# Chunk-selected attention into a softplus MLP on one core: constant rows cleared on GpSimd and written in pieces, key copies moved to GpSimd

## The chip, the cores and the metric

The kernel runs on one core of a Trainium2 chip. The metric is device time in microseconds (us); the time given for a kernel is the median over several runs, and one more execution is taken with the hardware profiler.

The engines are named here as the profile names them: PE is TensorE (PEld its weight loads), DVE is VectorE, ACT is ScalarE, POOL is GpSimd, SP is SyncE, which here issues DMAs alone.

## The reference

Inputs are q, k and v of shape 4 x 8 x 768 x 64 (batch, heads, tokens, head size), `w_in` of 512 x 2048 and `w_out` of 2048 x 512, all float32.

```
k_min, k_max = min, max of k over chunks of 32 tokens           # 24 chunks
ub    = sum_d max(q * k_min, q * k_max)                         # a bound for each query and chunk
ub    = -1e9 where the chunk lies after the query's own chunk
sel   = the 6 chunks with the largest ub, for each query
s     = q k^T / 8, kept where the key's chunk is in sel and the key is not after the query
attn  = softmax(s) v                                            # 4 x 8 x 768 x 64
x     = attn, heads side by side                                # 3072 x 512
out   = softplus(x w_in) w_out                                  # 3072 x 512
```

## The kernel before

**Blocks.** Work is cut into 12 blocks of 256 queries, three for each of the four batches, numbered n = 0 to 11. A block is prepared (`prep`), attended in four pairs of heads p = 0 to 3 (`attend`), and goes through the MLP (`mlp_h`, `mlp_y`). Blocks 0, 1 and 2 (all of batch 0) are the ramp: nothing else is there yet to fill TensorE. From block 3 on, preparation and attention of block n + 3 are interleaved with the MLP of block n.

**Preparation.** In the ramp, TensorE transposes k (L537) and q (L605) into PSUM; VectorE takes minimum and maximum over the chunks (`kx`, L544), copies them into a block-diagonal tile `bd` (L588) and makes the positive and negative parts of q (`qp`, `qn`, L624). TensorE multiplies these into the bounds (L646, L647). VectorE adds the causal mask (L653), takes the largest eight (L662), compares with the sixth (L672) and writes a mask row (L675); TensorE transposes it (L691) and it is copied beside q (`ma`, L696).

**Selection inside the score matmul.** The mask is applied by the score matmul itself. The tiles `ka` and `kb` (one of each for even and odd batches, `i` = 0 and 1) hold the keys of the two heads of a pair on 64 partitions and, on 32 more, one-hot rows that tell each key's chunk. `ka` uses partitions 0 to 63 for the keys and 64 to 95 for the one-hot rows; `kb` has zeros on partitions 0 to 31, the one-hot rows on 32 to 63 and the keys on 64 to 127. One matmul over them gives score plus penalty (L775). These rows are constant: zeros (`kb0`, L371), one-hot rows from the tile `ohb` (L374 for batch 0, a DMA on GpSimd's queue, L377, for batch 1).

**Blocks 0 and 1 are special** (`NSPLIT` = 2). Their keys go whole into `ka` of batch 1, which is still free, and their scores are made by half-height matmuls, keys first (L749) and the one-hot part from `ohb` itself (L756). Block 2 needs the keys of blocks 0 and 1 in the proper tiles of batch 0, so eight copies of 64 x 512 bring them there (`kcp`, L556). Block 2 reads them, and the constant rows of batch 0, when its scores (L775) begin.

**Attention.** ScalarE takes exponentials of the scores (L785), GpSimd clears the causal triangle (L791), TensorE multiplies with V (L802), VectorE inverts the sums (L811) and scales (L823). In the ramp TensorE transposes the result (L831) and a copy puts it into `x` (L836). V is cast from float32 by GpSimd or, in the ramp, by GpSimd or ScalarE, whichever the planner finds free (L721).

**MLP.** TensorE makes x w_in (L859), ScalarE softplus as exponential (L865) and logarithm (L869), TensorE multiplies with w_out (L885), VectorE copies it out (L890).

**Order.** Every step is a task with an engine, an estimated duration, a priority and the keys that it reads and writes. A planner (`Graph.schedule`) plays these through and fixes the order of instructions on each engine when the kernel is built; on the chip each engine runs its list in order and waits on semaphores. Where the planner sees TensorE without work in its first 30 us it writes a dummy matmul into the list (L387, 128 x 256). `at=` keeps a task from starting before a planned time, `port=True` says that a VectorE task may not overlap a GpSimd one in the plan, `MOVES` takes named tasks out of the finished order and puts them behind others. `RLEAD`, `POST`, `SHIFT`, `PLEAD` and `MSTART` shift priorities.

**DMA queues.** SP loads q, k and v. GpSimd's queue loads `w_in` in two pieces (L466) and `w_out` in four (L469); each group stands behind a one-element copy (`holdp`, L478) that waits for earlier loads.

In the old order, VectorE runs L371, both L374 and the eight L556 in one row after block 1's mask copy, and L371 for batch 1 soon after.

Of the kernel before, what the change touches and what calls it, by code (L numbers as in the profile page):

```python
# [9 lines left out]
F32 = mybir.dt.float32  # L10
# [10 lines left out]
NP = H // 2  # L21
# [11 lines left out]
NRAMP = 3  # L33
NSPLIT = 2
SWITCH = 0.1
CPP = -12
LATE = 22
W2 = 18
WARM = 30.0
COLD = 4.2  # L40
TD = 1.9
TLAT = 1.4
RLEAD = (0, 1, -3)
POST = (2, 5, 3)
OPRIO = 25
LEAD = 14
BG = 40
DMA_START = 1.3
MSTART = 18
AOFF = 8  # L50
PADD = 0.0
PLEAD = 18
AEND = 20
ORDER = "k0 q0 k1 v0 q1 v1 i01 i23 k2 q2 v2 o0 o1 o2 o3".split()
HOLDS = [("q", 1, 1), ("q", 2, 1), ("q", 2, 1)]

READS = [("q", 1, 0), ("k", 2, 1)]
MOVES = [("holdp", 0, "vc0", 1), ("ldw_in", 0, "holdp", 0), ("ohka", 0, "vc2", 1), ("ohkb", 0, "ohka", 0)]
SHIFT = (0, 0, 8)


OWN = {"PE": 0.0, "ACT": 0.05, "DVE": 0.07, "POOL": 0.05, "SP": 0.0}
# [20 lines left out]
class Graph:  # L83
# [7 lines left out]
    def add(self, eng, dur, fn, prio, r=(), w=(), dma=None, lat=None, name="", after=(), pkt=18, port=None, alt=None, at=0.0):  # L91
        t = Task()
        t.n, t.eng, t.dur, t.fn, t.prio, t.dma, t.name = len(self.tasks), eng, dur, fn, prio, dma, name
        t.lat = LAT[eng] if lat is None else lat
        t.pkt = pkt
        t.half = False
        t.port = port if port is not None else eng == "POOL" and dma is None
        t.alts = {eng: (dur, fn, t.port)}
        if alt:
            t.alts[alt[0]] = (alt[1], alt[2], False)  # L100
        deps, bufs = set(after), []
        for key in list(r) + list(w):
            b = key[0] if isinstance(key, tuple) else key
            if isinstance(b, Buf) and b not in bufs:
                bufs.append(b)
        for key in r:
            if key in self.last:
                deps.add(self.last[key])
            self.readers.setdefault(key, []).append(t)
        for key in w:  # L110
            if key in self.last:
                deps.add(self.last[key])
            deps.update(x for x in self.readers.pop(key, ()) if x is not t)
            self.last[key] = t
        t.deps, t.users, t.bufs = deps, [], bufs
        for d in deps:
            d.users.append(t)
        for b in bufs:
            b.left += 1
        t.wait, t.ready, t.start, t.end, t.order = len(deps), at, None, None, None  # L120
        self.tasks.append(t)
        return t
# [167 lines left out]
def build(nc, tiles):  # L290
# [77 lines left out]
    def background(i, pr, after, blks):  # L368
        add("DVE", 0.2, lambda: DV.memset(T("bd", i), 0.0), pr, w=[("bd", i)], name="bd0", after=after)
        add("DVE", 0.1, lambda: DV.memset(T("v", i)[:, :, :, D:D + 1], 1.0), pr, w=[("v1", i)], name="v1", after=after)  # L370
        add("DVE", 1.35, lambda: DV.memset(T("kb", i)[0:32], 0.0), CPP2 if i == 0 else pr + 2, w=[("kb0", i)], name="kb0", after=after, at=LATE if i == 0 else 0.0)  # L371
        for which in ("ka", "kb"):
            if i == 0:
                add("DVE", 0.9, lambda which=which: DV.tensor_copy(*oh(which, i, blks)), CPP2, at=LATE, r=["ohb"], port=True,  # L374
                    w=[(which + "c", i, k_) for k_ in blks], name="oh" + which + "0", after=after)
                continue
            add("POOL", 0.6, lambda which=which: PO.dma_start(*oh(which, i, blks)), pr, r=["ohb"],  # L377
                w=[(which + "c", i, k_) for k_ in blks], name="oh" + which, after=after, dma=0.8, pkt=200, lat=0.7)

    for i in range(2):  # L380
        add("DVE", 0.5, lambda i=i: DV.memset(T("mr", i), 0.0), -8, w=[("mr0", i)], name="mr0")
    CPP2 = when_att[2, 0] + CPP
    background(0, -6, (), [0, 1, 2])


# [128 lines left out]
    def prep(n):  # L514
# [13 lines left out]
        if ramp:  # L528
            for hh in range(2):
                kT = ps("t")  # L530
                p2 = slice(hh * 2, hh * 2 + 2)

                def tr(hh=hh, kT=kT):
                    for p in range(2):
                        for t in range(NT):
                            c0 = (p * NT + t) * 128
                            PE.transpose(T(kT)[:, c0:c0 + 128], columns("k", n, hh, p, t), T("identf"))  # L537
                add("PE", 0.44, tr, pr + 0.01 * hh, r=landing("k", n, hh) + ["identf"], w=[kT], name=f"kT{n}")

                def kab(which, rs, kT=kT, p2=p2):  # L540
                    AC.copy(T(which, i)[rs, p2, ks_], T(kT)[rs].rearrange("d (p s) -> d p s", p=2))

                def red(m, kT=kT, p2=p2):
                    DV.tensor_reduce(T(kx)[:, m, p2],  # L544
                                     T(kT).rearrange("d (p c s) -> d p c s", p=2, s=CH), axis=AX.X,
                                     op=ALU.max if m == 0 else ALU.min, negate=m == 1)
                kr = add("DVE", 1.26, lambda red=red: (red(0), red(1)), pr + 0.1, r=[kT], w=[(kx, m, hh) for m in range(2)],
                    name=f"kx{n}")
                if split:

                    def kae(kT=kT, p2=p2):
                        AC.copy(T("ka", 1)[:, p2, ks_], T(kT).rearrange("d (p s) -> d p s", p=2))
                    add("ACT", 0.5, kae, pr + 0.2, r=[kT], w=[("ka", 1, j, hh) for j in js] + [("kac", 1, blk, hh)],
                        name=f"ka{n}", after=[kr] if n == 0 else ())
                    for which, rs in (("ka", slice(0, 64)), ("kb", slice(64, 128))):
                        add("DVE", 0.24, lambda which=which, rs=rs, p2=p2: DV.tensor_copy(  # L556
                            T(which, i)[rs, p2, ks_], T("ka", 1)[rs, p2, ks_]), when_att[2, 0] + CPP, at=LATE, port=True,
                            r=[("ka", 1, j, hh) for j in js] + [("kac", 1, blk)], w=[(which, i, j, hh) for j in js], name=f"kcp{n}")
                    continue
                add("ACT", 1.06, lambda kab=kab: (kab("ka", slice(0, 64)), kab("kb", slice(64, 128))), pr + 0.2, r=[kT],  # L560
                    w=[(w_, i, j, hh) for w_ in ("ka", "kb") for j in js], name=f"ka{n}")
        else:
            ks = KQ["k", n]
            kt = Buf("kt")

            def tr(ks=ks, kt=kt):
                SP.dma_start_transpose(T(kt), T(ks).rearrange("s p t c -> s (p t c)"))
            add("SP", TD, tr, pr, at=pr - 4, r=[(ks, 0), (ks, 1)], w=[kt], dma=1.25, lat=TLAT, name=f"kTd{n}")
            for m in range(2):
                def red(m=m, kt=kt):  # L570
                    DV.tensor_reduce(T(kx)[:, m].rearrange("d p (t c) -> d p t c", t=NT),  # L571
                                     T(kt).rearrange("d (p t) (c s) -> d p t c s", t=NT, s=CH),
                                     axis=AX.X, op=ALU.max if m == 0 else ALU.min, negate=m == 1)
                add("DVE", 1.13, red, pr + 1, r=[kt], w=[(kx, m, 0), (kx, m, 1)], name=f"kx{n}")

            def kab(which, rs, kt=kt):
                DV.tensor_copy(T(which, i)[rs, :, ks_].rearrange("d p (t s) -> d p t s", t=NT),
                               T(kt)[rs].rearrange("d (p t) s -> d p t s", t=NT))
            add("DVE", 0.36, port=True, fn=lambda: kab("ka", slice(0, 64)), prio=pr + 4, r=[kt],
                w=[("ka", i, j, hh) for j in js for hh in range(2)], name=f"ka{n}")  # L580
            add("DVE", 0.36, port=True, fn=lambda: kab("kb", slice(64, 128)), prio=pr + 4, r=[kt],
                w=[("kb", i, j, hh) for j in js for hh in range(2)], name=f"kb{n}")
# [134 lines left out]
        if ramp:  # L717
            for t in range(NT):
                xv = XF["v", n, t]
                def vc(eng, xv=xv, t=t):  # L720
                    return lambda: (PO.tensor_copy if eng else AC.copy)(  # L721
                        v_dst(n, t), T(xv).rearrange("s (h d) -> s h d", h=H))
                add("POOL", 0.6, vc(1), pr + 2, r=[(xv, 0), (xv, 1)], w=[("v", i, blk * NT + t)], name=f"vc{n}",
                    alt=("ACT", 0.52, vc(0)))


    OALL = {}
# [1 line left out]
    def attend(n, p):  # L729
# [32 lines left out]
        for h in range(2):  # L762
            pt = Buf("pt")
            pts.append(pt)
            for j in range(0, t0 + 2, 2):
# [10 lines left out]
                                  qq[r0:r1, p, q0:QB], start=True, stop=True)  # L776
                kn = "ka" if h == 0 else "kb"
                hh = p // 2
                r = [(kn, i, j, hh), (kn, i, j + 1, hh), (kn + "c", i, j // 2)] + ([("kb0", i)] if h else [])
                r += [(qb, hh, z) for z in range(3)] if h else [(qa, hh, z) for z in range(3)]  # L780
                if not halves:
                    add("PE", 0.166 if last else 0.22, sm, pr_s, r=r, w=[sp], name=f"s{n}")
# [239 lines left out]
```

## Time and profile before

| | us |
|---|---|
| median of 7 runs | 259.41 |
| lowest and highest | 258.95, 260.42 |
| the profiled execution, its own time | 259.29 |
| its span, first to last instruction | 257.6 |
| TensorE busy | 251.2 |
| ScalarE busy | 199.2 |
| VectorE busy | 151.7 |
| GpSimd busy | 83.5 |

All durations below come from the one profiled execution. A row of the order of time gives start, duration, engine, line, operation, output and input, and how many instructions are merged; what stands in brackets is how long the engine sat idle before it and who ended the wait. Starts count from the span's start.

### The profile page before, as it was taken

Reading aid. Unit: us, or ns where it says so; the run is one execution under the profiler, and the core shown is the slowest. Engines: PE = TensorE matmul, PEld = TensorE weight load, DVE = VectorE, ACT = ScalarE, POOL = GpSimd, SP = SyncE. Lnnn points to the kernel's source line nnn. Section 1 sums busy time; section 2 is a strip of 40 time slices with the busy share of each in tenths; the row PEclk is TensorE's granted clock in tenths of the full one; section 3 lists DMA queues with packets and bytes.
Section 4 is the critical chain, followed back from the end, with each engine's and each line's share of the span. In section 5 each row is a group of like instructions: output and inputs, shape, how many; then the busy total and the mean of one; then the engine's idle time right before and its main releaser. Section 6 shows DMA issues by size and latency. Waiting matters only on the chain.

```text
span 257.6 us, 6836 instructions
## 1 busy us (share of the span) xinstructions
PE 251.2 (98%) x2620; PEld 189.1 (73%) x2620; DVE 151.7 (59%) x555; ACT 199.2 (77%) x359; POOL 83.5 (32%) x176
## 2 busy tenths in 40 slices
PE   8999899999999999999999999999999999999994
PEld 6887696687685786877687778677677687685763
DVE  5897958458876993949896229486487310221101
ACT  2677989988494999899389879769689679796570
POOL 3352460256063470458223244323523001010000
PEclk9999999999999999999999999999999999999999
DMA  8999899999986969999963599744992310111202
GB/s 181 272 194 216 185 160 186 253 190 276 154 216 148 225 166 187 226 174 242 195 163 84 131 220 246 165 120 102 227 189 33 92 43 1 43 41 41 84 0 83
DMA packets 119897, 39.64 MB, mean 154 GB/s; under 512 B 113496, under 2 KB 115800, under 8 KB 119864
## 3 DMA queue, kind: packets, MB, share of 16 engines
q1 hardware_dynamic: 114456, 34.09, 61.3%
q0 software_dynamic: 3296, 4.59, 10.2%
q10 hardware_dynamic: 2112, 0.52, 0.9%
q8 instruction: 20, 0.33, 0.6%
q14 instruction: 13, 0.11, 0.1%
HBM read 27.26 MB, written 6.29 MB: 130 GB/s over the span
## 4 chain that ended last, share of the span: by engine, by line
PE 92%; DVE 6%; issue 1%; ACT 0%; DVEq 0%
PE ps L885 32%; PE ps L859 31%; PE ps L775 12%; PE ps L802 7%; PE ps L387 5%; PE ps L537 1%; PE ps L605 1%; DVE kx L571 1%; PE ps L647 1%; PE ps L831 1%; DVE qpn L624 1%; PE ps L646 1%; DVE yo L890 1%; DVE ka L556 1%; PE ps L749 1%; PE ps L691 1%
## 5 line engine op out<-in xcount | busy, mean ns | idle before, releaser
L859 PE MATMUL ps<-x,w_in_sb 128*128 128x256 bf16 x768 | 100.9, 272 | 0.0
L785 ACT ACTIVATE pt<-ps 128x512 bf16<-128x512 f32 (+1 forms) x192 | 91.9, 560 | 7.7 <-PE ps L775 5.8
L885 PE MATMUL ps<-w_out_sb,g 128*128 128x512 bf16 (+1 forms) x400 | 97.2, 370 | 0.0
L859 PEld LDWEIGHTS <-w_in_sb 128*128 128x128 bf16 x768 | 72.0, 98 | 15.4 <-issue 0.7
L791 POOL TENSOR_SCALAR_AFFINE_SELECT pt<-pt 128x256 bf16<-128x256 bf16 x96 | 41.3, 438 | 127.9 <-ACT pt L785 127.9
L865 ACT ACTIVATE e<-ps 128x512 f32<-128x512 f32 x96 | 57.7, 616 | 30.3 <-PE ps L859 29.9
L885 PEld LDWEIGHTS <-g 128*128 128x128 bf16 x400 | 37.1, 98 | 25.0 <-ACT g L869 0.3
L869 ACT ACTIVATE g<-e 128x1024 bf16<-128x1024 f32 x48 | 51.4, 1071 | 1.1
L890 DVE COPY yo<-ps 128x512 f32<-128x512 f32 (+1 forms) x25 | 16.7, 667 | 43.7 <-PE ps L885 42.8
L811 DVE RECIPROCAL st<-ps 128x4 f32<-128x4 f32 x48 | 8.5, 178 | 36.9 <-PE ps L802 36.4
L802 PEld LDWEIGHTS <-pt 128*128 128x128 bf16 x672 | 26.5, 97 | 3.6
L802 PE MATMUL ps<-v,pt 128*128 128x65 bf16 x672 | 28.0, 193 | 0.0
L775 PE MATMUL ps<-qab,kb 128*128 128x256 bf16 (+1 forms) x168 | 25.8, 259 | 0.0
L775 PE MATMUL ps<-qab,ka 96*128 96x256 bf16 (+1 forms) x168 | 24.6, 259 | 0.0
L457 POOL CAST w<-w 128x512 bf16<-128x512 f32 x36 | 22.3, 635 | 4.6 <-DMA w<-in_q_dram 2.9
L571 DVE TENSOR_REDUCE kx<-w 128x32 bf16<-128x1024 bf16 x18 | 21.3, 1210 | 1.3 <-DMA w<-w 1.2
L775 PEld LDWEIGHTS <-ka 96*128 96x128 bf16 x168 | 15.4, 97 | 6.2 <-DVE qab L696 0.2
L775 PEld LDWEIGHTS <-kb 128*128 128x128 bf16 x168 | 14.7, 97 | 4.9
L387 PE MATMUL ps<-zero 128*128 128x256 bf16 x96 | 15.2, 294 | 1.1 <-DVE zero L355 1.1
L823 DVE TENSOR_TENSOR w<-ps,st 128x256 bf16<-128x256 f32 x36 | 15.2, 421 | 1.1
L662 DVE MAX8 ub<-ub 128x8 f32<-128x24 f32 (+2 forms) x160 | 14.2, 161 | 0.1
L455 POOL CAST v<-w 128x512 bf16<-128x512 f32 x18 | 11.4, 631 | 4.7 <-DMA w<-in_v_dram 4.7
(70 smaller groups left out, 181.9 us busy)
## 6 DMA issues: line engine op xcount, KB each, us to landing
w<-in_v_dram SPq DMA_DIRECT2D x24, 256.0 KB, 4.2
out_dram<-yo SPq DMA_DIRECT2D x23, 256.0 KB, 3.5
w<-in_k_dram SPq DMA_DIRECT2D x22, 256.0 KB, 3.8
w<-in_q_dram SPq DMA_DIRECT2D x22, 256.0 KB, 4.1
w_in_sb<-in_moe_w_in_dram POOLq DMA_DIRECT2D x2, 1024.0 KB, 11.0
w_out_sb<-in_moe_w_out_dram POOLq DMA_DIRECT2D x4, 512.0 KB, 8.7
w<-in_k_dram SPq DMA_DIRECT2D x2, 128.0 KB, 3.0
w<-in_k_dram ACTq DMA_DIRECT2D x2, 128.0 KB, 3.1
```

What stands on the lines that cost most here:

```text
L387: PE.matmul(T(Fill)[:, 0:256], T("zero")[:, 0:128], T("zero"), start=True, stop=True)
L457: PO.tensor_copy(T(b_)[:, :, t], T(xf).rearrange("s (p c) -> s p c", p=NP))
L571: DV.tensor_reduce(T(kx)[:, m].rearrange("d p (t c) -> d p t c", t=NT), T(kt).rearrange("d (p t) (c s) -> d p t c s", t=NT, s=CH), axis=AX ...
L775: PE.matmul(T(sp)[:, z * QB:z * QB + QB - q0], kk[r0:r1, p, (j + z) * 128:(j + z + 1) * 128], qq[r0:r1, p, q0:QB], start=True, stop=True)
L785: AC.activation(T(pt)[:, j:j + 2].rearrange("k j c -> k (j c)")[:, 0:w], T(sp)[:, 0:w], ACT.Exp, scale=SCALE)
L791: PO.affine_select(out=diag, in_=diag, compare_op=ALU.is_ge, fill=0.0, base=0, channel_multiplier=-1, pattern=[[0, 2], [1, 128]])
L802: PE.matmul(o[:, u, h], T(pts[h])[:, j, c0:c0 + 128], T("v", i)[:, j, 2 * p + h, :], start=(j == 0), stop=(j == t0 + u))
L859: PE.matmul(o, T("w_in")[:, dt, ft * 128:(ft + 1) * 128], T(x)[:, dt], start=(dt == 0), stop=(dt == KDM - 1))
L865: AC.activation(T(e)[:, f2 * 2:f2 * 2 + 2].rearrange("f a s -> f (a s)"), T(hp), ACT.Exp)
L869: AC.activation(T(gb)[:, f4 * 4:(f4 + 1) * 4], T(e), ACT.Ln, bias=1.0)
L885: PE.matmul(T(y)[:, 0:w], T(gb)[:, f, u * 128:(u + 1) * 128], T("w_out")[:, f, cs], start=(f == 0), stop=(f == KFF - 1))
L890: add("DVE", 0.06 + 0.54 / parts, lambda y=y, yo=yo, w=w: DV.tensor_copy(T(yo)[:, 0:w], T(y)[:, 0:w]), pr, r=[y], w=[yo], name=f"yo{n}")
```

## The change

The zero rows of `kb` of both batches are cleared by GpSimd, in the first microseconds, as 1536 float32 columns, in place of VectorE's L371. Batch 0's one-hot rows are written by VectorE in eight pieces of 768 columns, one for each tile and pair of heads, at a priority that puts them ahead of block 0's first reductions, in place of two copies of 3072. The score matmuls wait for the piece of their own pair. The eight key copies of blocks 0 and 1 become GpSimd's and stand behind its `w_out` loads. Block 1's V casts may no longer go to ScalarE. Seven of the planner's constants change, two are new (`KBP`, `OHP`), and one `MOVES` entry goes away.

In the two built orders this gives the following. On VectorE the eight pieces stand directly behind L370 and ahead of L544, and from block 1's mask copy on no constant rows or key copies are left. On GpSimd two memsets stand behind L330; both V casts of block 1 stand between masks of blocks 0 and 1; block 0's second V cast and its second mask copy (L696) are ScalarE's. The second `w_in` load stands behind two masks instead of six. Behind the four `w_out` loads come one V cast, one of the two one-hot DMAs of batch 1, the eight key copies, and the other DMA. TensorE's list has 99 dummy matmuls instead of 96; between the last transpose of block 0's q and its first L646 stand 17 of them and a group of k transposes, where 5 stood. Block 2's L646 groups and the first L885 stand earlier among the L859. From the middle of the schedule on the order of all engines differs in many places.

```diff
-CPP = -12
-LATE = 22
+CPP = 0
+KBP = 3
+OHP = 5
+LATE = 37
...
-RLEAD = (0, 1, -3)
-POST = (2, 5, 3)
+RLEAD = (1, 2, 3)
+POST = (6, 5, 0)
...
-MSTART = 18
+MSTART = 16
...
-PLEAD = 18
+PLEAD = 14
...
-MOVES = [("holdp", 0, "vc0", 1), ("ldw_in", 0, "holdp", 0), ("ohka", 0, "vc2", 1), ("ohkb", 0, "ohka", 0)]
-SHIFT = (0, 0, 8)
+MOVES = [("holdp", 0, "vc0", 1), ("ldw_in", 0, "holdp", 0), ("ohkb", 0, "vc2", 1)]
+SHIFT = (0, 0, 12)
...
-        add("DVE", 1.35, lambda: DV.memset(T("kb", i)[0:32], 0.0), CPP2 if i == 0 else pr + 2, w=[("kb0", i)], name="kb0", after=after, at=LATE if i == 0 else 0.0)
         for which in ("ka", "kb"):
             if i == 0:
-                add("DVE", 0.9, lambda which=which: DV.tensor_copy(*oh(which, i, blks)), CPP2, at=LATE, r=["ohb"], port=True,
-                    w=[(which + "c", i, k_) for k_ in blks], name="oh" + which + "0", after=after)
+                for p in range(NP):
+                    def piece(which=which, p=p):
+                        d, o = oh(which, i, blks)
+                        DV.tensor_copy(d[:, p], o[:, p])
+                    add("DVE", 0.26, piece, OHP, r=["ohb"], port=True, w=[(which + "c", i, k_, p) for k_ in blks],
+                        name="oh" + which + "0", after=after)
                 continue
...
-    CPP2 = when_att[2, 0] + CPP
+    for i in range(2):
+        add("POOL", 1.65, lambda i=i: PO.memset(T("kb", i)[0:32].rearrange("c p s -> c (p s)").bitcast(F32), 0.0), KBP,
+            w=[("kb0", i)], name="kb0")
...
-                        add("DVE", 0.24, lambda which=which, rs=rs, p2=p2: DV.tensor_copy(
-                            T(which, i)[rs, p2, ks_], T("ka", 1)[rs, p2, ks_]), when_att[2, 0] + CPP, at=LATE, port=True,
+                        add("POOL", 0.6, lambda which=which, rs=rs, p2=p2: PO.tensor_copy(
+                            T(which, i)[rs, p2, ks_], T("ka", 1)[rs, p2, ks_]), LATE + CPP, at=LATE,
...
-                    alt=("ACT", 0.52, vc(0)))
+                    alt=("ACT", 0.52, vc(0)) if n != 1 else None)
...
-                r = [(kn, i, j, hh), (kn, i, j + 1, hh), (kn + "c", i, j // 2)] + ([("kb0", i)] if h else [])
+                r = [(kn, i, j, hh), (kn, i, j + 1, hh), (kn + "c", i, j // 2), (kn + "c", i, j // 2, p)] + ([("kb0", i)] if h else [])
```

## The prediction

> **What bounds the kernel now.** I read the page first, then busy time by stretches, then the order of time of single engines where a stretch was not full.
>
> ```profile
> PE 251.2 (98%) x2620; PEld 189.1 (73%) x2620; DVE 151.7 (59%) x555; ACT 199.2 (77%) x359; POOL 83.5 (32%) x176
> ...
> PEclk9999999999999999999999999999999999999999
> ...
> PE 92%; DVE 6%; issue 1%; ACT 0%; DVEq 0%
> ```
>
> TensorE is busy 98% of the span at full clock, and the chain that ended last is TensorE for 92%. The change leaves TensorE's real matmuls alone. TensorE runs its queue in order, so the time is: its fixed work, plus the dummy matmuls (L387, fillers written into the order while TensorE has nothing ready in the ramp), plus the stalls where the next instruction's operand is late. Only the last two can move.
>
> The stretches show where the stalls are (columns: stretch, its length, then busy time of PE, PEld, DVE, ACT, POOL, then clock, DMA share, GB/s):
>
> ```profile
> 10.00:22.60 12.60, 12.60 (x178) 10.31 (x177) 10.82 (x57) 9.01 (x21) 5.55 (x13) 1.00 1.11 214
> 22.60:30.00 7.40, 6.38 (x88) 4.36 (x85) 6.94 (x15) 7.02 (x15) 3.09 (x6) 1.00 0.83 176
> 60.00:80.00 20.00, 19.84 (x200) 14.06 (x199) 16.89 (x71) 13.71 (x25) 9.17 (x18) 1.00 0.92 194
> 80.00:100.00 20.00, 19.65 (x206) 14.64 (x205) 14.57 (x50) 17.07 (x30) 8.25 (x15) 1.00 0.86 192
> 100.00:120.00 20.00, 19.80 (x247) 15.73 (x245) 14.73 (x45) 18.81 (x40) 10.24 (x21) 1.00 1.03 216
> ```
>
> One real hole lies at 22.6 to 30 us; three small ones (0.16, 0.35, 0.20) come later, and from 120 us on there is none. In order of time, TensorE:
>
> ```profile
> 7.51 0.73 PE L605 MATMUL ps<-identf,w 128*128 128x128 f32 x4
> 8.07 0.71 PE L387 MATMUL ps<-zero 128*128 128x256 bf16 x5
> 8.62 0.17 PE L646 MATMUL ps<-bd,qpn 128*128 128x16 bf16 x1
> ...
> 28.37 0.61 PE L859 MATMUL ps<-x,w_in_sb 128*128 128x256 bf16 x4
> 30.08 0.29 PE L831 MATMUL ps<-ident,osb 128*128 128x128 bf16 x2 [1.10 <-DVE osb L823]
> ```
>
> Five fillers step from 8.07 to 8.62, so one costs 0.109. The L859 matmuls have the same step: four from 28.37 are streamed by 28.81, and the next starts at 30.08. The hole is 1.27. VectorE around it and at the start:
>
> ```profile
> 3.27 0.10 DVE L370 MEMSET v<- 128x48 bf16 x1
> 4.98 2.48 DVE L544 TENSOR_REDUCE kx<-ps 128x16 bf16<-128x512 f32 x4 [1.61 <-PE ps L537]
> ...
> 24.27 0.95 DVE L374 COPY ka<-ohb 32x3072 bf16<-32x3072 bf16 x1
> 25.23 1.06 DVE L374 COPY kb<-ohb 32x3072 bf16<-32x3072 bf16 x1
> ...
> 27.32 0.29 DVE L556 COPY kb<-ka 64x512 bf16<-64x512 bf16 x1
> 27.62 0.51 DVE L556 COPY ka<-ka 64x512 bf16<-64x512 bf16 x1
> ...
> 29.18 0.18 DVE L811 RECIPROCAL st<-ps 128x4 f32<-128x4 f32 x1
> ```
>
> L811 had its product at about 25 (the L802 group before it began at 24.43) and stood behind the zeroing, the one-hot rows and the key copies from 22.91 to 29.15. And GpSimd:
>
> ```profile
> 3.06 0.29 POOL L330 TENSOR_SCALAR_AFFINE_SELECT ident<-ident 128x128 bf16<-128x128 bf16 x1
> 9.53 0.61 POOL L721 CAST v<-w 128x512 bf16<-128x512 f32 x1 [6.18 <-DMA w<-in_v_dram]
> ...
> 24.86 0.63 POOL L791 TENSOR_SCALAR_AFFINE_SELECT pt<-pt 128x256 bf16<-128x256 bf16 x1 [0.91 <-ACT pt L785]
> 25.73 0.83 POOL L791 TENSOR_SCALAR_AFFINE_SELECT pt<-pt 128x256 bf16<-128x256 bf16 x1 [0.25 <-ACT pt L785]
> ...
> 48.68 0.40 POOL L791 TENSOR_SCALAR_AFFINE_SELECT pt<-pt 128x256 bf16<-128x256 bf16 x1 [12.26 <-ACT pt L785]
> ```
>
> Read these against VectorE. An L791 alone takes 0.41. The one at 24.86 ran until the first L374 ended (25.22) plus 0.27; the one at 25.73 until the second ended (26.29) plus 0.27. In turn the second L374 took 0.11 longer than the first, and the L556 at 27.62, issued just after a L791 at 27.59, took 0.51 instead of 0.29. So a GpSimd instruction and such a VectorE copy exclude each other, and they **alternate**: the one that waits goes in between two back-to-back copies of the other.
>
> **The change, part by part.**
>
> *The hole at 30.08 goes: -1.27.* L371, L374 and L556 leave that stretch of VectorE (6.2 us), so L811 and L823 run on time. Next late there would be ScalarE (7.02 busy of 7.40): in the old order the last mask of block 1 ended at 31.69, and its L802 at 33.00 would move up to 31.73. It just fits, so I take all of it; the other end is 0.8.
>
> *Fillers: +0.33.* The built order has 99 instead of 96: 3 x 0.109.
>
> *The start.* The eight one-hot pieces now stand on VectorE right after L370 (3.37) and ahead of the reductions L544, and two GpSimd memsets of 32x1536 float32 follow L330. One memset: GpSimd's rows are 0.10 for one column and 0.206 for 128, so 0.83 ns a column and 1.38 us; the high end, by the casts' 0.61 for 512, is 1.83. One piece of 768 columns: 0.29 for 512 and 0.95 for 3072 give 0.15 + 0.26 ns a column, 0.35, and 0.365 from start to start; the low end is a quarter of L374, 0.24. No row shows a GpSimd memset beside such a copy; the ends are "no exclusion" and "full exclusion", and I take the second, by the nearest rows (L791 with L374). Then: memset one 3.30 to 4.68 (GpSimd's next row starts some 0.06 before the last one ends, 3.35); piece one was issued at 3.40, waits, ends 4.94; memset two goes in between, to 6.25; piece two ends 6.5; six more make 8.7. L544 starts at 8.7, not 4.98. Its 2.48, then L624, two L588 (0.37), and three more L624 (the four at 7.89 and 9.09 took 0.71) end at 12.3, and the second L646/L647 group ends at 12.45. TensorE comes there, by its order, after 17 fillers instead of 5 and one transpose group: 8.07 + 17 x 0.109 + 0.44 = 10.36, and would end the group at 10.57. Stall: **+1.85**, from +1.1 with the cheap pieces to +2.75 with the dear memset. Ten fillers after it cover mask work that needs them, and everything behind hangs on this chain, so nothing gives it back before the ramp ends. The Trainium skill speaks against this part too: "SBUF — State Buffer", section "Who interferes with whom", lets whichever of a two-port VectorE copy and a GpSimd instruction comes first keep the shared port for the whole instruction while the other blocks. The L791 rows above agree; for a memset no row of this run shows it. By that rule the start costs the stall just worked out, without it none.
>
> *Key copies on GpSimd: +0.5.* Eight copies of 64x512, by L457's 0.61 some 0.58 to 0.61 each, 4.7 in all, behind the w_out issues, one V cast and one DMA issue. In the old run those ended at 34.75, 35.37 and 35.87, and then GpSimd idled 12.3 us, so GpSimd has room. But VectorE runs block 2's chain there: the second of its reductions ended 3.9 after the transposes began (36.27 to 40.17), then L588 twice, L624. Without the start's stall the transposes begin at 36.27 - 1.27 + 0.33 = 35.3, and VectorE reaches L588 at 39.2. GpSimd, with the w_out issues where they were, ends its copies at 34.75 + 0.62 + 0.59 + 4.8 = 40.8. So 2 to 3 copies alternate with two L588 and two L624: up to 1.2 late. In the new order TensorE comes to this L646 after 16 transposes, 16 L859 and 8 L885, which is 1.74 + 1.75 + 1.73 = 5.2 after the first transpose, and VectorE alone would be through after 3.9 + 0.37 + 0.5 = 4.8: 0.4 in hand. That leaves 0 to 0.8 of stall; with the slip of the casts' duration on both sides I keep 0 to 1.0 and take 0.5. The scores that read the copies come some 4 us later.
>
> *Nothing, with the cover named.* Block 1's V casts on GpSimd (2 x 0.61) lie in its idle 6.13 us before 22.66; uncovered, they would delay the masks by up to 1.2. One V cast and one mask copy of block 0 go to ScalarE, which idled 1.69 before 10.55. The one-hot DMAs of batch 1: one waits behind the copies, its rows are first read near 70 us. The w_out pieces: they landed at 37.33, 40.14, 43.02 and 46.27, and the first matmul on them started at 40.20. Counted off in the new order from 35.3, their first uses come at 38.4, 41.2, 43.8 and 46.5, so 0.2 to 1.1 is left; uncovered, a later issue costs its own length beyond that. The later schedule is reordered; I leave its 0.71 of holes as it is, +-0.5.
>
> Sum on the profiled execution (259.29): -1.27 + 0.33 + 1.85 + 0.5 = +1.41, so 260.70; that execution is 0.12 below the median of the runs (259.41), which gives **260.8**. Its own range, with the bounds above, is 260.1 to 261.6.
>
> **The rivals.**
>
> *No exclusion (faster).* GpSimd's memset writes and reads nothing, and no row shows it holding up a copy. Then eight pieces run from 3.40 to 6.3, L624 to L647 are through by 10.1, before TensorE's 10.36: no stall. -1.27 + 0.33 + 0 to 0.5 gives 258.4 to 259.0. It decides when L544 starts before 6.9. Chance 0.22.
>
> *VectorE keeps the turn.* The second memset waits for all pieces: L544 at 4.68 + 2.9 = 7.6, stall 0.75, sum -0.2 to +0.3: 259.2 to 259.7. The L791 that slipped in between two copies speak against it. Chance 0.18.
>
> *w_out binds as well.* If its chunks land 1 us later than assumed, TensorE waits there too: 261.6 and more. Chance 0.08.
>
> The forecast has 0.52. That the change does not do what it says: only in part, since ScalarE gets rid of two V casts and gains one.
>
> **How the numbers follow.** 0.3% (0.78 us) is about what a measurement here can tell from no change. Faster (below 258.63): 0.17 of the first rival and 0.01 of the forecast, 0.18. Same: 0.05, 0.17 and 0.04, 0.26. Slower (above 260.19): 0.47, 0.08 and 0.01, 0.56. The range 258.7 to 261.5 leaves about 0.13 below and 0.07 above.
>
> **What would show it.** Right: L544 starts near 8.7 with VectorE's pieces of up to 1.5 us among ones of 0.35; TensorE stalls 1.5 to 2 us before L646 near 10.4; no hole of over 0.5 before L831 between 24 and 34; L588 and L624 of block 2 stretched beside GpSimd copies. Wrong: L544 before 7, or the old hole still there with another releaser.

## The result, and the profile after

| | before | changed |
|---|---|---|
| median (us) | 259.85 | 261.38 |
| lowest and highest | 258.76, 262.05 (47 runs) | 260.08, 262.13 (20 runs) |
| ratio, 95% interval | | 1.0058 [1.0044, 1.0072] |
| the profiled execution, and its span | 259.29, 257.6 | 262.36, 260.6 |

The changed kernel is 0.58% slower, some 1.5 us. Its profiled execution lies 1.0 us above the median of its runs and above every one of the 20, so single stalls in it can be larger than is usual.

From L387 on, the changed kernel's line numbers are 7 higher: L551 is the reduction that was L544, L653 was L646, L892 was L885. Its one-hot copies are L378, its memsets L388. The first lines of the page that moved, the busy time and the chain that ended last:

```profile
PE 253.0 (97%) x2623; PEld 189.7 (73%) x2623; DVE 152.5 (58%) x550; ACT 198.1 (76%) x359; POOL 91.5 (35%) x187
...
PE 72%; DMA 9%; DVE 9%; ACT 6%; POOL 2%; issue 1%; SPq 0%; DVEq 0%; ACTq 0%
```

TensorE carried 92% of that chain before and carries 72% now; DMA, VectorE and ScalarE have come into it. The stretches (same columns as before):

```profile
10.00:22.60 12.60, 11.85 (x157) 9.52 (x156) 10.86 (x59) 8.54 (x21) 6.76 (x14) 1.00 1.09 204
22.60:30.00 7.40, 7.40 (x123) 5.55 (x122) 3.81 (x18) 6.71 (x15) 2.27 (x6) 1.00 0.95 200
30.00:48.00 18.00, 17.61 (x182) 13.48 (x177) 11.75 (x48) 15.80 (x28) 10.78 (x19) 1.00 0.99 175
48.00:60.00 12.00, 11.62 (x150) 9.29 (x147) 4.02 (x11) 10.13 (x22) 5.24 (x11) 1.00 1.04 212
```

The old hole at 22.6 to 30 us is gone: 7.40 busy of 7.40 where it was 6.38. In its place the ramp before it, full until now, misses 0.75, and two later stretches miss 0.39 and 0.38. The start, VectorE, then GpSimd, then TensorE in order of time:

```profile
3.39 3.61 DVE L378 COPY ka<-ohb 32x768 bf16<-32x768 bf16 x4
7.01 1.16 DVE L378 COPY kb<-ohb 32x768 bf16<-32x768 bf16 x4
8.18 2.49 DVE L551 TENSOR_REDUCE kx<-ps 128x16 bf16<-128x512 f32 x4
```

```profile
3.30 2.68 POOL L388 MEMSET kb<- 32x1536 f32 x2
```

```profile
10.02 0.60 PE L544 MATMUL ps<-identf,w 128*128 128x128 f32 x4
11.13 0.17 PE L653 MATMUL ps<-bd,qpn 128*128 128x16 bf16 x1 [0.51 <-DVE bd L595]
...
11.77 0.64 PE L544 MATMUL ps<-identf,w 128*128 128x128 f32 x4
```

The first four pieces took 3.61 us, the other four 1.16. Taken singly, the first piece lasted from 3.39 to 6.20, 2.81 us, until both memsets (1.37 each) were through; the others start 0.27 apart. So the reductions begin at 8.18 where they began at 4.98. TensorE comes to L653 at 10.46 (10.02 and four steps of 0.109) and could have ended the group of eight at 10.67; it ends at 11.77: a stall of 1.1.

The key copies run on GpSimd from 37.62 to 43.07, and VectorE's chain for block 2 runs beside them (first row before, second row now); TensorE then waits here, for w_out, and for block 3:

```profile
40.69 0.98 DVE L624 TENSOR_SCALAR qpn<-qab 128x512 bf16<-128x512 bf16 x4
```

```profile
41.65 1.77 DVE L631 TENSOR_SCALAR qpn<-qab 128x512 bf16<-128x512 bf16 x4
```

```profile
42.45 0.20 PE L653 MATMUL ps<-bd,qpn 128*128 128x48 bf16 x1 [0.24 <-DVE qpn L631]
...
49.49 1.02 PE L892 MATMUL ps<-w_out_sb,g 128*128 128x512 bf16 x4 [0.38 <-DMA w_out_sb<-in_moe_w_out_dram]
...
65.98 0.28 PE L838 MATMUL ps<-ident,osb 128*128 128x128 bf16 x2 [0.40 <-DVE osb L830]
```

Measured from the start of the matmul before less that one's usual step, these stalls are 0.40, 0.55 and 0.56; the matmul after the first of them loses 0.17 more, and 0.39 goes at 63.95. The four L631 took 0.98 before and take 1.77. Why w_out is late is in GpSimd's order (its w_out issues before, then its last rows now), and what hangs on it in SyncE's:

```profile
31.76 2.99 POOL L469 DMA_DIRECT2D w_out_sb<-in_moe_w_out_dram  x4
```

```profile
33.06 0.41 POOL L798 TENSOR_SCALAR_AFFINE_SELECT pt<-pt 128x256 bf16<-128x256 bf16 x1 [0.46 <-ACT pt L792]
...
33.54 2.99 POOL L476 DMA_DIRECT2D w_out_sb<-in_moe_w_out_dram  x4
```

```profile
45.32 0.60 SPq L491 DMA_DIRECT2D scratch<-w_out_sb  x1
```

The four w_out issues stand behind block 1's last mask. That mask was at 31.28 and is at 33.06, 1.78 later; the pieces landed at 37.33, 40.14, 43.02 and 46.27 before and land at 39.06, 41.94, 45.30 and 49.45 now. And SyncE's one-element copy of w_out waits for the third piece (it started at 43.04 before, 0.02 after the landing, as it starts at 45.32 now); behind it stand all loads of q, k and v for the blocks from 3 on. SyncE issued its second pair of k loads after it at 55.57 before and at 59.42 now.

The profile shows one thing more. Block 2's last V load has landed at 34.00, and w_out is only issued from 33.54 on, so the DMA engines run dry: their share of busy time (the column DMA share) between 31 and 36 us is 0.50 (0.94 before), and between 36 and 46 us it is 1.18 (1.16 before). What did not move in that gap moves later: the last w_out piece is issued 1.78 later and lands 3.18 later. In the experiments below the share between 31 and 36 us is 0.57, 0.53 and 0.54 in experiments 1, 2 and 4, and 1.12 and 1.13 in 3 and 5, where two of the w_out loads go sooner. No run changes the gap alone.

### The profile page after: what moved, and what is told of

Its sections match the earlier page's. It is cut to its first block, busy times and chain, and to the rows that moved or that the text cites. A ratio compares the mean times of both kernels' runs of the same rounds, so it can differ in the third digit from the quotient of the medians.

```text
span 260.6 us, 6841 instructions
## 1 busy us (share of the span) xinstructions
PE 253.0 (97%) x2623; PEld 189.7 (73%) x2623; DVE 152.5 (58%) x550; ACT 198.1 (76%) x359; POOL 91.5 (35%) x187
## 4 chain that ended last, share of the span: by engine, by line
PE 72%; DMA 9%; DVE 9%; ACT 6%; POOL 2%; issue 1%; SPq 0%; DVEq 0%; ACTq 0%
PE ps L892 28%; PE ps L866 26%; PE ps L782 10%; PE ps L809 6%; DMA w_out_sb<-in_moe_w_out_dram 5%; DMA w<-in_v_dram 4%; ACT pt L792 4%; DVE kx L551 2%; DVE ka L378 1%; ACT e L872 1%; DVE qpn L631 1%; POOL w_out_sb L476 1%; POOL v L462 1%; PE ps L654 1%; ACT g L876 1%
## 5 line engine op out<-in xcount | busy, mean ns | idle before, releaser
L892 PE MATMUL ps<-w_out_sb,g 128*128 128x512 bf16 (+1 forms) x400 | 97.3, 370 | 0.4 <-DMA w_out_sb<-in_moe_w_out_dram 0.4
L798 POOL TENSOR_SCALAR_AFFINE_SELECT pt<-pt 128x256 bf16<-128x256 bf16 x96 | 40.0, 424 | 120.6 <-ACT pt L792 120.0
L892 PEld LDWEIGHTS <-g 128*128 128x128 bf16 x400 | 37.0, 98 | 25.5 <-issue 0.7
L782 PE MATMUL ps<-qab,kb 128*128 128x256 bf16 (+1 forms) x168 | 26.7, 259 | 0.0
L464 POOL CAST w<-w 128x512 bf16<-128x512 f32 x36 | 23.1, 662 | 4.2 <-DMA w<-in_k_dram 3.8
L782 PE MATMUL ps<-qab,ka 96*128 96x256 bf16 (+1 forms) x168 | 24.1, 259 | 0.1
L782 PEld LDWEIGHTS <-ka 96*128 96x128 bf16 x168 | 15.4, 97 | 5.4 <-issue 0.6
L782 PEld LDWEIGHTS <-kb 128*128 128x128 bf16 x168 | 14.8, 97 | 5.7
```

The costliest lines, as they stand in the source:

```text
L464: PO.tensor_copy(T(b_)[:, :, t], T(xf).rearrange("s (p c) -> s p c", p=NP))
L782: PE.matmul(T(sp)[:, z * QB:z * QB + QB - q0], kk[r0:r1, p, (j + z) * 128:(j + z + 1) * 128], qq[r0:r1, p, q0:QB], start=True, stop=True)
L798: PO.affine_select(out=diag, in_=diag, compare_op=ALU.is_ge, fill=0.0, base=0, channel_multiplier=-1, pattern=[[0, 2], [1, 128]])
L892: PE.matmul(T(y)[:, 0:w], T(gb)[:, f, u * 128:(u + 1) * 128], T("w_out")[:, f, cs], start=(f == 0), stop=(f == KFF - 1))
```

## The experiments

The question is which of the new stalls make the 1.5 us, and where the 1.27 us of the closed hole went. An entry of `MOVES` reads: the k-th task of this name goes behind the j-th task of that name. Ratios are to the kernel before, run on the same chip in the same job (medians of before 260.36, 260.00 and 260.01 in the three jobs).

**1. The memsets away from the pieces.** Changed kernel plus:

```diff
+ ("kb0", 0, "vc0", 0), ("kb0", 0, "ldw_in", 0)   # in MOVES
```

> The changed kernel, with GpSimd's two memsets set apart from VectorE's pieces: one behind the first V cast (near 10 us), one behind the first w_in issue (near 12.4 us), where VectorE has no fast copies. All else stands where it stood. Exclusion theory: the eight pieces run from 3.4 to about 5.7, L551 starts there instead of 8.18, and TensorE does not stall before L653 (near 10.5, 1.1 us lost in the changed kernel's trace), so about 1.1 us less than the changed kernel: 260.3, 0.2% over the kernel before. Rival, hidden by the ramp: later waits of the ramp (ScalarE, w_out) hold TensorE anyway, and the block 2 transposes still begin near 36.8: under 0.4 less. Rival, reordering: the loss lies in the stalls past 60 us: no change, 261.4.

Median 260.58, ratio 1.0009 [0.9990, 1.0028], 0.49% under the changed kernel's. The reductions start right behind pieces that none holds up:

```profile
5.73 2.48 DVE L551 TENSOR_REDUCE kx<-ps 128x16 bf16<-128x512 f32 x4
```

TensorE's start stall is gone. The later stalls stay (0.40 before L653 at 41.16, 0.40 at w_out, 0.59 at 62.78 and 0.55 at 64.82). So the encounter of memsets and pieces cost some 1.3 us of the total; by the two intervals, 0.7 to 1.9.

**2. The key copies spread between block 1's masks.**

```diff
+ ("kcp0", 0, "cm1", 1), ("kcp0", 1, "cm1", 3), ("kcp0", 2, "cm1", 5), ("kcp0", 3, "kcp0", 2)
```

> The changed kernel, with four of GpSimd's eight key copies moved ahead, into its idle time between the masks of block 1 (one near 25.8, one near 27.7, two near 30.2); four stay behind the w_out issues and should end near 40.3, before VectorE's L595 of block 2. Theory that the copies hold up VectorE: the two L595 and four L631 of block 2 fall from 0.75 and 1.77 us back to about 0.37 and 0.98, the 0.40 us before L653 near 42.4 goes, 0.4 us less in all: 261.0. Rival, w_out comes next: TensorE is 0.4 us sooner at the last w_out piece and waits there that much longer: no change. Rival, the copies now hold up the masks of block 1: slower.

Median 261.45, ratio 1.0042 [1.0027, 1.0058]. The stall at 42 went, but the waits behind it grew to about 1.16 and 1.04:

```profile
49.18 1.02 PE L892 MATMUL ps<-w_out_sb,g 128*128 128x512 bf16 x4 [0.99 <-DMA w_out_sb<-in_moe_w_out_dram]
```

```profile
65.86 0.28 PE L838 MATMUL ps<-ident,osb 128*128 128x128 bf16 x2 [0.88 <-DVE osb L830]
```

(They were 0.55 and 0.56; the 0.39 at 63.95 and the 0.31 before L782 went as well.) What TensorE won at 42 and 47 it mostly lost to w_out and to block 3's loads; 0.16% is left, inside the intervals.

**3. Two of the four w_out loads ahead of block 1's last two masks.**

```diff
+ ("holdp", 1, "cm1", 5), ("ldw_out", 0, "holdp", 1), ("ldw_out", 1, "ldw_out", 0)
```

> The changed kernel, with the wait ahead of the w_out loads and the first two of the four issues moved ahead of the last two masks of block 1, about 2.4 us sooner (31.1 instead of 33.5, held by the q load of block 2). w_out theory: the last piece lands near 46 to 47 instead of 48.0 to 49.5, the wait of 0.4 to 0.6 us before L892 at 49.5 goes: 0.4 to 0.6 us less, 260.9. Rival, the wait only shifts to the next late thing (V of the next block, scores): no change.

Median 260.33, ratio 0.9996 [0.9971, 1.0021]: 0.62% under the changed kernel, 1.6 us and more than the stall at w_out alone. That stall is gone, and so are those at 64 and 66 but for 0.19, and the one before L653 near 42 but for 0.14; the one before L782 grew from 0.31 to 0.56. SyncE's second pair of k loads went at 56.27, not 59.42. The lateness of w_out thus cost twice: once itself, once through the loads behind it.

**4. The kernel before, with nothing but the zero rows moved to GpSimd's first microseconds.**

```diff
-DV.memset(T("kb", i)[0:32], 0.0)
+PO.memset(T("kb", i)[0:32].rearrange("c p s -> c (p s)").bitcast(F32), 0.0)
+ ("kb0", 0, "ident", 0), ("kb0", 1, "kb0", 0)   # in MOVES
```

TensorE's, ScalarE's and SyncE's orders are those of before.

> The kernel before with one part of the change alone: both zeroings of kb go to GpSimd, behind its start-up work (3.3 to 6 us), where the old order has VectorE in reductions from PSUM. The one-hot rows and the key copies stay on VectorE near 24 to 29 us. Theory: VectorE's row of constants gets 1.34 us shorter, L811 runs at about 27.85, and the hole of 1.27 us before L831 near 30 closes; nothing at the start gets later: 258.6, 0.5% less than the kernel before. Rival, ScalarE: it is the next bound at 24 to 36 us and keeps TensorE waiting for the exponentials: under 0.4 us less. Rival, exclusion reaches the first L588 and L624: slower by up to 0.5.

Median 260.87, ratio 1.0022 [1.0007, 1.0036]. My expectation of 258.6 failed. The hole is closed, and yet (TensorE, then VectorE):

```profile
29.97 0.28 PE L831 MATMUL ps<-ident,osb 128*128 128x128 bf16 x2
...
72.77 0.49 PE L775 MATMUL ps<-qab,ka 96*128 96x256 bf16 x4 [1.08 <-DVE qab L713]
```

```profile
69.93 2.35 DVE L571 TENSOR_REDUCE kx<-w 128x32 bf16<-128x1024 bf16 x2 [3.69 <-DMA w<-w]
```

In the kernel before, the first of these rows came at 30.08, after 1.10 of idling. The profiled execution is the slowest of the twelve, 0.8 us above their median. In it the ramp had started 1.1 us late, the closed hole took that back (block 2's transposes at 36.26, before 36.27), but the masks on GpSimd kept the delay: w_out was issued at 32.90 (31.76 before), SyncE's second pair of k loads at 58.23 (55.57), and TensorE lost 1.25 at 71.4: its mask copy L713 stood behind VectorE's L571, which waited for the transpose of those k loads and began at 69.93 (65.86 before). The hole had only ever held TensorE: block 1's last scores (L756, at 28.06 before) stand ahead of it, and the chain of masks, w_out and loads did not pass through it.

**5. The two together: kernel 4 with the two w_out loads sooner.**

> The kernel before with its zero rows cleared by GpSimd at the start (that alone closed the hole before L831 and still took 260.87, ratio 1.0022) and two of the w_out loads ahead of the last two masks of block 1. Theory 'what the hole gave was lost behind w_out': SyncE's loads for the later blocks wait for w_out, w_out's issue waits for the masks, and the masks never waited for the hole, so closing it only moved the stall to 71 us; with w_out sooner the gain stays: ratio 0.995 to 0.997 (259.0 to 259.5). Rival 'the memsets cost it at the start': the ramp's first transposes were 0.8 to 1.1 us late in that run's profile; then the ratio stays at 1.000 to 1.002 (260.3 to 260.9) and the profile shows the slip again.

Median 258.76, ratio 0.9955 [0.9934, 0.9977]: faster than the kernel before and than the changed one. The late start showed in this profile too (see the last section), so by itself it is not what had cost kernel 4 its gain. Whether the early memsets cost kernel 4 something besides is not separated by any run. The wait at 72 is gone:

```profile
71.38 0.49 PE L775 MATMUL ps<-qab,ka 96*128 96x256 bf16 x4
```

SyncE's one-element copy hardly moved (43.73; 43.95 in kernel 4), so what the early issue brought is not that the copy came sooner. What moved is the landings: the last w_out piece at 46.39 instead of 48.88, the first pair of k loads behind it at 51.75 in kernel 4 and at 49.15 here. This fits the gap in the DMA engines' work between 31 and 36 us, which is there in kernel 4 (0.54) and not here (1.13).

**6. The kernel before with w_out sooner alone.**

> The kernel before with nothing but two of the w_out loads ahead of the last two masks of block 1. Theory: its loads landed in time for TensorE and the hole before L831 hides the rest; at most the 0.30 us stall at 62 us goes: ratio 0.9985 to 1.000. Rival 'the loads behind w_out bind before as well': ratio 0.996 or less.

Median 260.08, ratio 1.0006 [0.9983, 1.0029]. With the hole open, an early w_out brings nothing; in this profile the hole is 1.62 and the wait before L831 at 63.34 is 0.64 (0.30 before). The two edits are worth 1.2 us together and nothing apart.

**7. The changed kernel with moves 1 and 3.**

> The changed kernel with two moves together: the GpSimd memsets away from the one-hot pieces (alone worth 1.3 us) and two of the four w_out loads ahead of the last two masks of block 1 (alone worth 1.6 us). Theory 'two separate losses': they add, ratio to the kernel before 0.994 to 0.996 (about 259.0 on a scale on which before takes 260.3). Rival 'one loss seen twice': both moves only bring the same later loads (SyncE's q, k and v loads for block 3 and on, which stand behind the landing of w_out) forward, so the second adds little: ratio 0.998 to 1.000 (259.8 to 260.3).

Median 260.49, ratio 1.0024 [0.9995, 1.0053]: not the sum, and no better than either alone. GpSimd, then TensorE:

```profile
42.25 0.61 POOL L728 CAST v<-w 128x512 bf16<-128x512 f32 x1 [8.61 <-DMA w<-in_v_dram]
```

```profile
46.69 0.56 PE L782 MATMUL ps<-qab,ka 96*128 96x256 bf16 x4 [0.45 <-POOL ka L563]
```

The early w_out held up block 2's last V load, which landed at 42.20 (34.00 in the changed kernel). The load had been issued only 0.30 before the first w_out piece; in experiment 3 it was 1.08 before it and landed at 36.78. On GpSimd the eight key copies stand behind that V cast, so they began at 43.37. The scores waited 0.57 at 45.87 for a mask copy (VectorE's L679 beside the key copies took 0.60 and 1.15 in place of 0.24) and 0.61 at 46.69 for the key copies themselves. In kernel 5 the same load landed as late (41.58), but its key copies were on VectorE long before.

**8. Moves 1, 2 and 3.**

> The two moves above and the key copies spread between the masks as well. Theory: with w_out early, the 0.40 us that the spread saved and lost again to w_out is now kept, ratio 0.001 to 0.0015 under that of the two moves (258.7). Rival: the copies between the masks delay the masks and with them ScalarE's and the loads' order; ratio equal or higher.

Median 259.58, ratio 0.9983 [0.9957, 1.0009]. Four of the eight copies now ran before 31.9, the V load landed at 37.45 with its cast at 37.51, the other four followed from 38.62, and 0.15 is left of the stalls before L782. That fits the reading of 7, though it is no clean test of it, since the V load came sooner too. The changed kernel with all three moves is level with the kernel before; its median is 0.8 us above kernel 5's, but the intervals overlap.

**9. Each memset cut in three, back to back.**

```diff
+            for z in range(3):
+                PO.memset(t[:, 512 * z:512 * (z + 1)], 0.0)
```

> The changed kernel with each of the two GpSimd memsets cut into three of 512 columns, so six stand back to back at the start instead of two; nothing else is moved. Theory 'GpSimd keeps its turn over memsets that follow each other': the first one-hot piece (issued at 3.39) still ends only after the last memset, at about 6.2, and the reductions still start at about 8.2. Rival 'they alternate, and the changed kernel's second memset got in by chance of timing': the first piece ends after the first or second third, between 4.1 and 4.7, other pieces of 0.6 to 0.9 lie among the thirds.

One execution, 261.47. VectorE and GpSimd (here L391 is the memset that was L388):

```profile
3.38 3.13 DVE L378 COPY ka<-ohb 32x768 bf16<-32x768 bf16 x4
```

```profile
3.29 3.69 POOL L391 MEMSET kb<- 32x512 f32 x6
```

Neither theory as I put it. Singly, the first piece ended at 4.48, just after two memsets of 0.51; from there on memsets of 0.73 and pieces of 0.75 took turns, until the memsets ended at 6.98. So the first copy was passed by the memset that ran and by one more, and then they alternated. In the changed kernel there were only two memsets.

**10. One memset at the start, the other behind the first w_in load.**

```diff
+ ("kb0", 1, "ldw_in", 0)
```

> The changed kernel with only one memset at the start; the second is moved behind the first w_in load. Theory 'the pieces wait for whatever memset has begun': the first piece ends at 4.9 to 5.0, the others step by 0.27, the reductions start at about 6.9 and TensorE has no stall before L653 near 10.4 (1.1 with both memsets first). Rival 'any memset ahead costs the start': a stall of 0.4 or more stays there.

One execution, 260.40. The first piece ended at 4.87, the reductions began at 6.86, and TensorE, which came to L653 at 10.70, did not wait there. The 1.1 us thus came from the second memset.

**11. Kernel 5 with the memsets in GpSimd's idle time after block 0's masks.**

```diff
-("kb0", 0, "ident", 0)
+("kb0", 0, "cm0", 7)
```

> The kernel before with the zero rows cleared by GpSimd in its idle time after block 0's last mask (about 16.5 to 19.3 us) rather than in the first microseconds, and two w_out loads ahead of the last two masks of block 1. Theory 'closing the hole pays once w_out is sooner, wherever the zeros are written': ratio 0.993 to 0.997 as with the memsets at the start (0.9955). Rival 'memsets at the start cost the ramp something' (the first transposes ran at half pace until 6.4 to 6.9 us in three of five profiles with early memsets, until 4.3 to 5.5 in the five without): 0.991 to 0.993. Rival 'VectorE's copies of 16 to 19 us collide with the memsets there': above 0.997.

Median 261.38, ratio 1.0065 [1.0040, 1.0090]: the third theory, at a price that I had not foreseen. VectorE and TensorE:

```profile
16.50 2.95 DVE L624 TENSOR_SCALAR qpn<-qab 128x512 bf16<-128x512 bf16 x1
```

```profile
19.51 0.21 PE L646 MATMUL ps<-bd,qpn 128*128 128x32 bf16 x1 [2.14 <-DVE qpn L624]
```

An instruction that took 0.32 before took 2.95, from the end of a mask through both memsets (16.60 to 19.30), and TensorE stood for 2.3 us. Part of the price is the clock: in four of the twelve executions, the profiled one among them, the granted clock is 0.993, and these took 262.06 to 264.08; the other eight took 260.33 to 261.85, still above the 260.01 of the kernel before. Idle time of GpSimd is no free place if VectorE has such an instruction there.

## Why the prediction was right or wrong

The time (260.8 against 261.38), its side and the main mechanism, that memsets and pieces hold each other up and TensorE waits for it, were right. Against the kernel before, 1.4 us were forecast and 1.53 measured. That the sum came so near is luck in part: the start was priced 0.75 too dear, and w_out, the stalls behind it and the V casts, priced at nothing, made up for it. Of the signs named, the hole went and block 2's L588 and L624 were stretched, as said; L544's start (8.18 for 8.7), the longest piece (2.81 for 1.5) and the stall (1.1 for 1.5 to 2) had other sizes.

Two things in the sum don't hold up. The range "260.1 to 261.6" is not what the bounds give: added up, they run from 259.1 to 263.2. And the terms below are measured in one execution of each kernel; these two differ by 3.07 us, twice what the medians differ by, so the measured terms do not add up to the 1.53.

**The hole.** As a stall it went, all of it. As a term of the total it was mis-priced: experiments 4 to 6, all on the kernel before, show that closing it by early memsets is worth nothing while w_out comes where it came, and 1.2 us once w_out comes sooner. The step that failed is "I take all of it", which looked for what is late next on ScalarE and in the masks, and not in the loads.

**The start: mis-sized, 1.85 for 1.1.** The exclusion, its place, the memset's duration (1.38 estimated, 1.37 measured) and TensorE's arrival (10.36 estimated, 10.46 measured) were right. Wrong was that memset and pieces alternate from the first turn on, and that each piece needs 0.365: both memsets went first and the pieces then stepped by 0.27, so the reductions began at 8.18 and not at 8.7. From there the chain needed 3.6 where I had 3.75. The rivals "no exclusion" and "VectorE keeps the turn" are both out; it was GpSimd that kept the turn.

The page "SBUF — State Buffer" of the Trainium skill, section "Who interferes with whom", which the prediction weighed, names `tensor_scalar` beside copies among those that can take the shared ports; experiment 11's L624 agrees (0.32 to 2.95). The section says that "Whoever issues first gets the shared pair for the whole instruction" and does not say what a second instruction in the queue does. Taken for one instruction at a time, the waiting copy would have followed the first memset; here it followed the second, in experiment 9 too, and the measurement decides.

**Key copies: 0.5 for 0.57** (0.40 before L653 and 0.17 at the matmul after it), as forecast. There was a further 0.31 before L782 at 47.04, which I had dismissed with "some 4 us later"; in experiment 2, with the copies spread, all of it went.

**w_out: mis-sized, 0 for 0.55,** and with it the later stalls. I moved the first uses earlier by the closed hole and left the landings where they were. But the issues stand behind the masks and the masks behind the ramp's start: the last mask came 1.78 later and the landings 1.7 to 3.2 later. The start is most of that and not all: in experiment 1, without its stall, the w_out issues still began at 32.25, 0.49 after the kernel before. What the last piece lost beyond that fits the gap in the DMA engines' work. The rival "w_out binds as well", at 0.08, was the mechanism at work, with 0.55 where it had 0.8 or more. What "I leave its 0.71 of holes as it is" did not see are SyncE's loads behind w_out: the stalls between 62 and 66 us were 0.30 and are 0.95. (The 0.71 is what the busy time shows of those holes; counted by steps, the kernel before lost 0.30, 0.52 and 0.35 there.)

**V casts: 0 for 0.2.** The cover named was GpSimd's idle time, and GpSimd had it. But the two casts met two small VectorE casts (L682) that took 0.60 each in place of 0.17, and TensorE waited 0.21 before 21.48. I had asked what the casts delay on their own engine, and not on VectorE.

The fillers were as counted. In the profiled execution the stalls named here and the hole and fillers add up to about 2.4 of the 3.07 us between the two profiles; most of the rest is a wait of 0.69 at 120.4 (for a V load, by way of a GpSimd cast ahead of a mask), which the profiles of experiments 1 to 3 do not have in this size, and small steps that I did not trace.

## What to carry to other kernels

A hole is worth its length only if everything late at its end also passed through it: before pricing one, follow the queues that don't (here masks, then a weight load on GpSimd's queue, then every later load on SyncE's), see whether the DMA engines run dry meanwhile, and ask whether these would be the next to be late. When work is moved to an idle engine, list what the engine that it can hold up does in those microseconds, and count the instructions that stand back to back there. And two edits that each bring nothing can be worth over a microsecond together, so an edit that closes a hole and yet brings no time should be tried again with the next wait relieved.

## What the runs showed of the hardware

- A VectorE copy or `tensor_scalar` issued while GpSimd worked back to back was passed not only by the instruction that ran but by one more (2.81 us in the changed kernel, 1.10 with short memsets) or by two (2.95 us, experiment 11: the end of a mask and both memsets); after that, where more followed, the engines took turns instruction by instruction.
- In the first microseconds the fillers step by 0.213 us, and from some moment on by 0.109, while the profile's granted clock reads 1.00 throughout. Over 13 profiles the first short step ended between 4.6 and 7.2 us (before 5.2, changed 5.6, experiment 4 6.7, experiment 5 7.1). Eight fillers that took 1.04 in the kernel before took 1.57 in experiment 5, from 5.81 on. This is the late start of experiments 4 and 5. The three latest (6.7, 7.1 and 7.2) have both memsets at the start, but the changed kernel and experiment 2 have them too and switched at 5.6 and 5.0, so whether the memsets matter is open. The page "TensorE: Matmul & The Clock Gate" of the Trainium skill, section "Part 1: The HAM clock gate (the "warmup" mystery)", describes a free-running activity window of 3.4 us whose phase moves the switch by 0.5 us either way; the two rates that its formula gives for 256 columns, an estimate, 0.213 and 0.109, agree; the scatter here, 2.6 us, is wider.
- After the stall of 2.3 us in experiment 11 the fillers stepped by 0.21 again; there the profile does show it, a granted clock of 0.88 between 10 and 22.6 us.
